# Attention with decay, then a spectral mix, on one core: v loaded with two neighbouring keys per partition

## The chip, the core and the metric

The kernel runs on one core of one Trainium2 chip. The metric is the device time of one launch in microseconds (us). The kernel before the change took 465.24 us (median of three runs, 464.25 to 465.59).

## What is computed

There are two stages. The first is causal attention with a decay, for 8 batches and 8 heads, 576 positions and a head width of 64. The second works on its output x of shape 8 x 576 x 512.

```
scores = scale * q @ k.T                       # per batch and head
cum    = cumsum(log(clip(f, 1e-4, 1)))
scores = where(causal, -1e9, scores + cum[i] - cum[j])
x      = softmax(scores) @ v
X = rfft(x, axis=1); Y = X[:, :64] times (w_r + i*w_i), 512 x 512 per mode
u = x + irfft(Y);  out = u + relu(u @ w_ch)
```

The decay splits into a factor of the query and a factor of the key. The query's factor falls out of the softmax, so the kernel multiplies each row of v by exp(-cum[j]) and carries that weight itself as a 65th column. This column gives the sum that the rows are divided by.

## The kernel before

**Data.** The spectral weights w_r and w_i are 134 MB in HBM. They are cast to bf16 on the way in and make 128 loads of 512 KB at their destination. q, k and v are 9.4 MB each in HBM; q and k are cast, v stays in float32. All loads but f and the first few of v are issued by GpSimd (POOL), which works strictly in the order of the program. At most eight of its loads are under way at once in the trace.

**Pairs.** The attention is worked in 32 pairs (one batch, two heads, `hp` = 0 or 1), one per turn of the loop from L441 on, in a hand-written software pipeline. In turn i:

- POOL issues `load_qk(i + 3)` (L100: one load for q, one for k), `load_v(i + 3)` (L111: one load per head of keys 0 to 511 into `vt`, and for every fourth batch one per head of the last 64 keys of four batches into `vl`), and in most turns `issue_w()` (L140: w_r and w_i of one chunk, 512 KB each). Turns 4, 9, 10, 13 and 21 issue no chunk of w.
- DVE scales v of pair i + 1 (`scale_v`, L304), at the head of the turn.
- TensorE (PE) makes the scores of pair i (`scores`, L319, in parts 0 to 3), multiplies the exponentials of pair i - 1 with v (`av`, L376, blocks 0 to 4), and transposes q and k of pair i + 1 (`trans`, L285). These are interleaved: scores 0, av 0 and 1, scores 1, av 2, trans 0, scores 2, av 3, trans 1, scores 3, av 4. Then come the DFT of pair i - 2 (`dft`, L406) and, from turn 10 on, eight matmuls of one chunk of w (`spec_early`, L424), which frees that chunk's buffer.
- ScalarE (ACT) makes the exponentials of each part of the scores (L346, L333), DVE masks the diagonal blocks (`mask`, L348) and divides (`norm`, L392).

The five key blocks hold 128 consecutive keys each, the last one 64. A diagonal block is masked by the triangle `trimask`. The exponentials of a pair are three tiles of 2 x 512 columns plus a small one for the last block, and both heads' small blocks lie in one tile, heads on different partitions.

**Buffers.** Four of `qk` and of `vt`, two of `vl` (each serves four pairs), seven of w. A load waits until the last reader of its buffer is done.

**After the pairs** a loop over 16 groups of modes takes the remaining chunks of w (L581), each followed by the next `issue_w()`, and the output is made and stored (L634 to L668).

Of the kernel before, what the change touches and what calls it, by code (L numbers as in the profile page):

```python
# [23 lines left out]
def kernel(  # L24
# [11 lines left out]
    nc = tc.nc  # L36
# [34 lines left out]
    trimask = const.tile([128, 128], BF16, name="trimask")  # L71
    tri4 = const.tile([128, 2, 64], BF16, name="tri4")
# [6 lines left out]
    wT = const.tile([128, NPAIR, 9], F32, name="wT")  # L79
# [8 lines left out]
    vspool = actx.enter_context(tc.tile_pool(name="vspool", bufs=3))  # L88
    qtkt = actx.enter_context(tc.tile_pool(name="qtkt", bufs=2))
    epool = actx.enter_context(tc.tile_pool(name="epool", bufs=2))  # L90
# [7 lines left out]
    VG = 4  # L98
# [12 lines left out]
    def load_v(i):  # L111

        g, b = pairs[i]
        vt = vpool.tile([128, 8, Dh], F32, tag="vt", name="vt")
        st[i]["vt"] = vt
        q_v = nc.sync if i < 3 else nc.gpsimd
        for hp in range(2):
            q_v.dma_start(  # L118
                vt[:, 4 * hp : 4 * hp + 4, :],
                v[b, 2 * g + hp, 0:512, :].rearrange("(c p) d -> p c d", p=128),  # L120
            )
        if b % VG == 0:
            vl = vlpool.tile([128, VG, Dh], F32, tag="vl", name="vl")
            for hp in range(2):
                q_v.dma_start(
                    vl[64 * hp : 64 * hp + 64, :, :],
                    v[b : b + VG, 2 * g + hp, 512:576, :].rearrange("b p d -> p b d"),
                )
            for n in range(VG):
                st[i + n]["vl"] = vl[:, n, :]  # L130
# [52 lines left out]
    nc.sync.dma_start(ft, f.rearrange("b h s -> (b h) s"))  # L183
    load_qk(0)
# [6 lines left out]
    masks.make_upper_triangular(nc, trimask[:], val=1.0, diag=True)  # L191
# [35 lines left out]
    nc.vector.tensor_copy(cum[:, S : S + 64], cum[:, 512:576])  # L227
    cps = psM.tile([128, NSB, BH], F32, tag="m", name="cps")
    for sc in range(NSB):
        nc.tensor.transpose(  # L230
            cps[:, sc, :], cum[:, sc * 128 : sc * 128 + 128], ident_f[:BH, :BH]
        )
    for sc in range(4):
        for hp in range(2):
            nc.scalar.activation(
                wT[:, :, 4 * hp + sc].rearrange("p (g b) -> p b g", g=4),
                cps[:, sc, :].rearrange("p (b g hp) -> p b g hp", b=B, g=4)[:, :, :, hp],
                ACT.Exp,
                scale=-1.0,
            )  # L240
    for hp in range(2):
        nc.scalar.activation(
            wT[64 * hp : 64 * hp + 64, :, 8].rearrange("p (g b) -> p b g", g=4),
            cps[64 * hp : 64 * hp + 64, 4, :].rearrange("p (b g hp) -> p b g hp", b=B, g=4)[:, :, :, hp],
            ACT.Exp,
            scale=-1.0,
        )

    def setup_small():
        nc.vector.memset(tri4[:], 0.0)  # L250
        nc.vector.tensor_copy(tri4[0:64, 0, :], trimask[0:64, 0:64])
        nc.vector.tensor_copy(tri4[64:128, 1, :], trimask[64:128, 64:128])
# [51 lines left out]
    def scale_v(i):  # L304
        vs = vspool.tile([128, 9, Dh + 1], BF16, tag="vs", name="vs")
        st[i]["vs"] = vs
        nc.vector.tensor_tensor(  # L307
            vs[:, 0:8, 0:Dh], st[i]["vt"][:], _strided(wT[:, i, 0:8], [[1, 8], [0, Dh]]), ALU.mult
        )
        nc.vector.tensor_scalar(vs[:, 8, 0:Dh], st[i]["vl"], wT[:, i, 8:9], None, ALU.mult)  # L310
        nc.vector.tensor_copy(vs[:, :, Dh : Dh + 1], _strided(wT[:, i, :], [[1, 9], [1, 1]]))
# [3 lines left out]
        [(1, 128, 448, 0), (0, 512, 64, 448)],  # L315
        [(2, 256, 320, 0), (3, 384, 192, 320)],
    ]

    def scores(i, T):  # L319

        QT, KT = st[i]["T"][:, 0, :], st[i]["T"][:, 1, :]
        if T == 0:
            st[i]["et"] = epool.tile([128, 3, 2, 512], BF16, tag="et", name="et")
            st[i]["e4"] = epool.tile([128, 64], BF16, tag="e4", name="e4")
            st[i]["m4"] = epool.tile([128, 2, 64], BF16, tag="m4", name="m4")
        if T == 3:
            ps = psM.tile([128, 64], F32, tag="m", name="s4")
            for hp in range(2):
                sl = slice(64 * hp, 64 * hp + 64)
                nc.tensor.matmul(  # L330
                    ps[sl, :], lhsT=KT[sl, 512:576], rhs=QT[sl, 512:576], start=True, stop=True
                )
            nc.scalar.activation(st[i]["e4"][:], ps[:], ACT.Exp, scale=scale)  # L333
            return
        ps = psS.tile([128, 2, 512], F32, tag="S", name="sps")
        for jb, i0, n, c in SPANS[T]:
            for hp in range(2):
                sl = slice(64 * hp, 64 * hp + 64)
                nc.tensor.matmul(  # L339
                    ps[:, hp, c : c + n],  # L340
                    lhsT=KT[sl, jb * 128 : jb * 128 + 128],
                    rhs=QT[sl, i0 : i0 + n],
                    start=True,
                    stop=True,
                )
        nc.scalar.activation(st[i]["et"][:, T, :, :], ps[:], ACT.Exp, scale=scale)  # L346

    def mask(i, part):  # L348
        et = st[i]["et"]
        if part == 0:  # L350
            d = et[:, 0:2, :, 0:128]
            nc.vector.tensor_tensor(d, d, _strided(trimask[:], [[0, 2], [0, 2], [1, 128]]), ALU.mult)
        else:
            d = _strided(et[:, 2, :, 0:128], [[512, 2], [320, 2], [1, 128]])
            nc.vector.tensor_tensor(d, d, _strided(trimask[:], [[0, 2], [0, 2], [1, 128]]), ALU.mult)
            nc.vector.tensor_tensor(
                st[i]["m4"][:], _strided(st[i]["e4"][:], [[0, 2], [1, 64]]), tri4[:], ALU.mult
            )

    def eblk(i, hp, jb, sb):  # L360

        et = st[i]["et"]
        n = SBLK[sb]
        if jb == 4:
            return st[i]["m4"][:, hp, :]
        if jb == 0:
            T, c = (0, sb * 128) if sb < 4 else (1, 448)
        elif jb == 1:
            T, c = 1, (sb - 1) * 128
        elif jb == 2:  # L370
            T, c = 2, (sb - 2) * 128
        else:
            T, c = 2, 320 + (sb - 3) * 128
        return et[:, T, hp, c : c + n]

    def av(i, sb):  # L376
        if sb in (0, 3):
            st[i]["pav"] = psV.tile([128, 3, 2, Dh + 1], F32, tag="av", name="pav")
        pav, vs = st[i]["pav"], st[i]["vs"]
        Ms = SBLK[sb]  # L380
        for hp in range(2):
            for jb in range(sb + 1):
                rhs = vs[:, 8, :] if jb == 4 else vs[:, 4 * hp + jb, :]
                nc.tensor.matmul(  # L384
                    pav[:Ms, sb % 3, hp, :],
                    lhsT=eblk(i, hp, jb, sb),
                    rhs=rhs,
                    start=(jb == 0),
                    stop=(jb == sb),
                )  # L390

    def norm(i, part):  # L392
        g, b = pairs[i]
        pav = st[i]["pav"]
        for ns, lo, hi in ([(128, 0, 3)] if part == 0 else [(128, 3, 4), (64, 4, 5)]):
            n = hi - lo
            rcp = normsb.tile([128, 3, 2, 1], F32, tag="rcp", name="rcp")
            nc.vector.reciprocal(rcp[:ns, 0:n, :, :], pav[:ns, lo % 3 : lo % 3 + n, :, Dh : Dh + 1])
            nc.vector.tensor_tensor(  # L399
                x_all[:ns, g, b, lo:hi, :].rearrange("p s (h d) -> p s h d", h=2),  # L400
                pav[:ns, lo % 3 : lo % 3 + n, :, 0:Dh],
                _strided(rcp[:ns, 0:n, :, :], [[2, n], [1, 2], [0, Dh]]),
                ALU.mult,
            )
# [33 lines left out]
    scale_v(0)  # L438
    setup_small()
    spec_done = 0  # L440
    for i in range(NPAIR + 2):  # L441
# [6 lines left out]
        if i + 1 < NPAIR:  # L448
            scale_v(i + 1)
        prev = i - 1 if 1 <= i <= NPAIR else None  # L450
        if live:
            scores(i, 0)
        if prev is not None:
            av(prev, 0)
            av(prev, 1)
        if live:
            scores(i, 1)
        if prev is not None:
            av(prev, 2)
            norm(prev, 0)  # L460
        if i + 1 < NPAIR:
            trans(i + 1, 0)
        if live:
            scores(i, 2)
            mask(i, 0)
        if prev is not None:
            av(prev, 3)
        if i + 1 < NPAIR:
            trans(i + 1, 1)
        if live:  # L470
            scores(i, 3)
        if prev is not None:
            av(prev, 4)
            norm(prev, 1)
# [224 lines left out]
```

## Time and profile before

| | |
|---|---|
| time, median of 3 runs | 465.24 us |
| the profiled execution: its own time | 461.9 us |
| its span, first to last instruction | 460.1 us |
| granted TensorE clock over the span | 0.829 |
| PE, DVE, ACT, POOL busy | 75%, 53%, 49%, 42% of the span |
| bytes moved by the DMA engines | 96.64 MB |
| HBM read / written | 163.73 / 9.44 MB |

Shares of busy time are averages over three stretches: the pairs (to about 222 us), the main loop over w (to about 420 us) and the output. The DMA line of the page gives, for 40 equal slices, how busy the 16 DMA engines were in tenths. GB/s counts bytes at the destination, so a cast load counts half of what it reads. In a table of stretches the DMA share can be over 1, because packets overlap on one engine.

### The profile page before, as it was taken

Reading aid. Unit: us, or ns where it says so; the run is one execution under the profiler, and the core shown is the slowest. Engines: PE = TensorE matmul, PEld = TensorE weight load, DVE = VectorE, ACT = ScalarE, POOL = GpSimd, SP = SyncE. Lnnn points to the kernel's source line nnn. Section 1 sums busy time; section 2 is a strip of 40 time slices with the busy share of each in tenths; the row PEclk is TensorE's granted clock in tenths of the full one; section 3 lists DMA queues with packets and bytes.
Section 4 is the critical chain, followed back from the end, with each engine's and each line's share of the span. In section 5 each row is a group of like instructions: output and inputs, shape, how many; then the busy total and the mean of one; then the engine's idle time right before and its main releaser. Section 6 shows DMA issues by size and latency. Waiting matters only on the chain.

```text
span 460.1 us, 8535 instructions
## 1 busy us (share of the span) xinstructions
PE 344.0 (75%) x3396; PEld 169.6 (37%) x3396; DVE 245.2 (53%) x630; ACT 223.4 (49%) x332; POOL 192.3 (42%) x277
## 2 busy tenths in 40 slices
PE   1685897797977769686887479767964787977994
PEld 1353554454544435444433223322331232332331
DVE  7694687797756567677632212111120355533786
ACT  5575466586875658655522022012201354643774
POOL 9654675766566674655432223223232322200000
PEclk9997559798888789778989577577677699988998
DMA  9999999999999999999999999999999999994698
GB/s 167 212 226 212 198 209 225 210 204 190 222 216 210 222 203 223 218 218 218 205 206 206 206 207 206 206 207 206 207 207 206 207 206 207 206 206 70 218 326 279
DMA packets 89319, 96.64 MB, mean 210 GB/s; under 512 B 8288, under 2 KB 82528, under 8 KB 89280
## 3 DMA queue, kind: packets, MB, share of 16 engines
q0 software_dynamic: 80560, 85.61, 107.8%
q1 hardware_dynamic: 8720, 10.50, 7.2%
q8 instruction: 26, 0.43, 0.4%
q14 instruction: 13, 0.11, 0.1%
HBM read 163.73 MB, written 9.44 MB: 376 GB/s over the span
## 4 chain that ended last, share of the span: by engine, by line
DMA 69%; PE 13%; POOL 7%; DVE 5%; issue 5%; DVEq 0%; ACT 0%; POOLq 0%
DMA w<-in_moe_w_i_dram 52%; DMA vt<-in_v_dram 5%; DMA w<-in_moe_w_r_dram 4%; POOL vt L118 3%; DMA x_all<-in_moe_w_i_dram 3%; PE U L645 2%; DMA qk<-in_q_dram 2%; POOL w L152 2%; DMA qk<-in_k_dram 2%; PE Z L645 2%; POOL qk L106 2%; DVE qkT L299 2%; PE pav L384 2%; PE U L651 1%; PE sps L339 1%
## 5 line engine op out<-in xcount | busy, mean ns | idle before, releaser
L346 ACT ACTIVATE et<-sps 128x1024 bf16<-128x1024 f32 x96 | 95.4, 1042 | 19.5 <-PE sps L339 19.3
L152 POOL DMA_DIRECT2D w<-in_moe_w_r_dram x61 | 46.0, 754 | 77.6 <-DMA w<-in_moe_w_r_dram 29.6
L163 PE MATMUL A<-w,XS 128*32 128x512 bf16 x488 | 46.3, 444 | 36.6 <-DMA w<-in_moe_w_i_dram 24.4
L152 POOL DMA_DIRECT2D w<-in_moe_w_i_dram x61 | 46.2, 758 | 63.1 <-DMA w<-in_moe_w_i_dram 58.5
L537 ACT CAST XW<-pxw 128x512 bf16<-128x512 f32 (+1 forms) x40 | 23.3, 584 | 97.2 <-PE pxw L530 97.2
L384 PE MATMUL pav<-vs,et 128*128 128x65 bf16 (+1 forms) x896 | 58.5, 210 | 0.0
L384 PEld LDWEIGHTS <-et 128*128 128x128 bf16 (+1 forms) x896 | 42.2, 111 | 28.4 <-issue 26.4
L299 DVE COPY qkT<-tp 128x640 bf16<-128x640 bf16 x64 | 49.0, 766 | 4.8 <-PE tp L294 4.8
L118 POOL DMA_DIRECT2D vt<-in_v_dram x58 | 45.2, 786 | 11.9 <-DMA w<-in_moe_w_i_dram 3.8
L592 DVE TENSOR_TENSOR Yb<-A,yacc 128x512 bf16<-128x512 f32 x16 | 11.1, 692 | 73.2 <-PE A L163 73.2
L418 ACT CAST XS<-pd 128x192 bf16<-128x192 f32 x32 | 33.2, 1045 | 32.0 <-PE pd L411 31.9
L339 PE MATMUL sps<-qkT 64*128 64x512 bf16 (+4 forms) x320 | 45.0, 347 | 3.9 <-ACT et L346 2.1
L307 DVE TENSOR_TENSOR vs<-vt,wT 128x512 bf16<-128x512 f32 x32 | 22.1, 690 | 47.2 <-DMA vt<-in_v_dram 47.2
L530 PE MATMUL pxw<-wch,xT 128*128 128x512 bf16 (+1 forms) x160 | 46.5, 453 | 0.0
L294 PE MATMUL tp<-ident_bf,qk 128*64 128x128 bf16 x576 | 32.8, 249 | 14.7 <-DMA qk<-in_k_dram 13.1
L399 DVE TENSOR_TENSOR x_all<-pav,rcp 128x384 bf16<-128x384 f32 (+2 forms) x96 | 36.2, 377 | 3.4
L576 DVE TENSOR_TENSOR XW<-pz,XW 128x512 bf16<-128x512 f32 (+1 forms) x40 | 27.0, 690 | 20.2 <-PE pz L575 19.9
L521 DVE COPY xT<-ptr 128x576 bf16<-128x576 bf16 x32 | 14.6, 458 | 36.5 <-PE ptr L516 36.3
L106 POOL DMA_DIRECT2D qk<-in_k_dram x32 | 19.8, 619 | 32.5 <-DMA w<-in_moe_w_i_dram 29.1
L163 PEld LDWEIGHTS <-XS 128*32 128x32 bf16 x512 | 10.3, 96 | 56.7 <-issue 51.1
L662 DVE SCALAR_TENSOR_TENSOR o_sb<-Z,u_sb 128x512 f32<-128x512 f32 (+1 forms) x40 | 25.7, 685 | 8.4 <-ACT u_sb L661 7.5
L294 PEld LDWEIGHTS <-qk 128*64 128x64 bf16 x576 | 21.5, 124 | 20.2 <-DMA qk<-in_q_dram 8.3
(106 smaller groups left out, 502.1 us busy)
## 6 DMA issues: line engine op xcount, KB each, us to landing
w<-in_moe_w_r_dram POOLq DMA_DIRECT2D x61, 512.0 KB, 19.8
w<-in_moe_w_i_dram POOLq DMA_DIRECT2D x61, 512.0 KB, 19.7
out_dram<-o_sb SPq DMA_DIRECT2D x16, 512.0 KB, 3.3
vt<-in_v_dram POOLq DMA_DIRECT2D x58, 128.0 KB, 7.8
qk<-in_q_dram POOLq DMA_DIRECT2D x32, 144.0 KB, 9.6
qk<-in_k_dram POOLq DMA_DIRECT2D x32, 144.0 KB, 8.4
x_all<-in_moe_w_r_dram POOLq DMA_DIRECT2D x3, 512.0 KB, 8.8
x_all<-in_moe_w_i_dram POOLq DMA_DIRECT2D x3, 512.0 KB, 9.9
```

What stands on the lines that cost most here:

```text
L106: nc.gpsimd.dma_start(qk[64 * n : 64 * n + 64, :, :], src[b, 2 * g : 2 * g + 2, :, :].rearrange("h (p r) d -> p h (r d)", p=64),)
L118: q_v.dma_start(vt[:, 4 * hp : 4 * hp + 4, :], v[b, 2 * g + hp, 0:512, :].rearrange("(c p) d -> p c d", p=128),)
L152: nc.gpsimd.dma_start(w8[:, t, :, :], src[4 * u : 4 * u + 4, dc * 128 : (dc + 1) * 128, :].rearrange("m p e -> p m e"),)
L163: nc.tensor.matmul(A[32 * j : 32 * j + 32, :], lhsT=XS[:, dc, c0 : c0 + 32], rhs=w8[:, t, j, :], start=(first and t == 0), stop=(last and ...
L294: nc.tensor.transpose(tp[64 * hp : 64 * hp + 64, r - r0, :, :].rearrange("p n c -> p (n c)"), qk[:, hp, r * 64 : r * 64 + 64], ident_bf[:, :],
L299: nc.vector.tensor_copy(st[i]["T"][:].rearrange("p n (c r) -> p n c r", r=9)[:, :, :, r0:r1], tp[:, 0 : r1 - r0, :, :].rearrange("p r n c ...
L339: nc.tensor.matmul(ps[:, hp, c : c + n], lhsT=KT[sl, jb * 128 : jb * 128 + 128], rhs=QT[sl, i0 : i0 + n], start=True, stop=True,)
L346: nc.scalar.activation(st[i]["et"][:, T, :, :], ps[:], ACT.Exp, scale=scale)
L384: nc.tensor.matmul(pav[:Ms, sb % 3, hp, :], lhsT=eblk(i, hp, jb, sb), rhs=rhs, start=(jb == 0), stop=(jb == sb),)
L399: nc.vector.tensor_tensor(x_all[:ns, g, b, lo:hi, :].rearrange("p s (h d) -> p s h d", h=2), pav[:ns, lo % 3 : lo % 3 + n, :, 0:Dh], _stri ...
L418: nc.scalar.copy(XS[:, g, 0 : 24 * NM].rearrange("p (m c b) -> p c m b", c=3, b=8)[:, :, :, b], pd[:])
L530: nc.tensor.matmul(pxw[:Ms, :], lhsT=xT[:, eb, sb * 128 : sb * 128 + Ms], rhs=wch[:, eb, :], start=(eb == 0), stop=(eb == NEB - 1),)
```

## The change

The keys of v are laid out differently, and the key blocks follow.

- **Loads of v.** Each partition gets two neighbouring keys, so a row of the load is 512 B instead of 256 B: block 0 holds the even keys of 0 to 255, block 1 the odd ones, blocks 2 and 3 the same of 256 to 511. The last 64 keys are loaded for two batches at a time (`VG = 2`), rows of 256 B as before, and both heads go to partitions 64 to 127.
- **Scores.** The weights of a scores matmul are every second column of the transposed k. A block of even or odd keys spans 256 positions, so more columns are computed (3712 instead of 3200 per pair, both heads together). The last keys' block is taken with 128 keys (448 to 575), of which v's rows for the first 64 are zero. It is part of part 2, and the small separate block goes. There are four exponentials per pair: 1024, 1024, 896 and 768 columns.
- **Masks** cover 256 columns of each block (`tri2`), and 64 columns of the last (`trit`).
- **av** has 34 matmuls per pair instead of 30, all 128 rows wide; `norm` divides the last two blocks in one go (four instructions per pair instead of six).
- **Order.** Scores 0 and 1 are put together, then av 0 to 2, both transposes, scores 2 and 3, av 3 and 4. `scale_v(i)` moves into turn i, behind `mask(i, 0)`; before it was done a turn earlier, at the head of turn i - 1.
- The exponentials and the scaled v live in two fixed tiles each (`ets`, `vss`), used in turn, instead of pools of two and three.

```diff
-    VG = 4
+    VG = 2
+    ets = [ssb.tile([128, 4, 2, 512], BF16, name=f"et{n}") for n in range(2)]
+    vss = [ssb.tile([128, 10, Dh + 1], BF16, name=f"vs{n}") for n in range(2)]
...
-                vt[:, 4 * hp : 4 * hp + 4, :],
-                v[b, 2 * g + hp, 0:512, :].rearrange("(c p) d -> p c d", p=128),
+                vt[:, 4 * hp : 4 * hp + 4, :].rearrange("p (s r) d -> p s (r d)", s=2),
+                v[b, 2 * g + hp, 0:512, :].rearrange("(s p r) d -> p s (r d)", s=2, r=2),
...
-            vl = vlpool.tile([128, VG, Dh], F32, tag="vl", name="vl")
+            vl = vlpool.tile([128, VG, 2, Dh], F32, tag="vl", name="vl")
             for hp in range(2):
                 q_v.dma_start(
-                    vl[64 * hp : 64 * hp + 64, :, :],
+                    vl[64:128, :, hp, :],
...
-    masks.make_upper_triangular(nc, trimask[:], val=1.0, diag=True)
+    nc.gpsimd.affine_select(out=tri2[:], in_=tri2[:], ...)
+    nc.gpsimd.affine_select(out=trit[:], in_=trit[:], ...)
...
+    KEYS = [slice(0, 256, 2), slice(1, 256, 2), slice(256, 512, 2), slice(257, 512, 2), TAIL]
     SPANS = [
         [(0, 0, 512, 0)],
-        [(1, 128, 448, 0), (0, 512, 64, 448)],
-        [(2, 256, 320, 0), (3, 384, 192, 320)],
+        [(1, 0, 512, 0)],
+        [(2, 256, 320, 0), (1, 512, 64, 320), (4, 512, 64, 384)],
+        [(3, 256, 320, 0), (0, 512, 64, 320)],
     ]
...
-                    lhsT=KT[sl, jb * 128 : jb * 128 + 128],
+                    lhsT=KT[sl, KEYS[blk]],
...
-            nc.vector.tensor_tensor(d, d, _strided(trimask[:], [[0, 2], [0, 2], [1, 128]]), ALU.mult)
+        d = et[:, 2 * part : 2 * part + 2, :, 0:256]
+        nc.vector.tensor_tensor(d, d, _strided(tri2[:], [[256, 2], [0, 2], [1, 256]]), ALU.mult)
+        if part == 1:
+            d = et[:, 2, :, 384:448]
+            nc.vector.tensor_tensor(d, d, _strided(trit[:], [[0, 2], [1, 64]]), ALU.mult)
...
-        if i + 1 < NPAIR:
-            scale_v(i + 1)
         if live:
             scores(i, 0)
+            scores(i, 1)
         if prev is not None:
             av(prev, 0)
             av(prev, 1)
-        if live:
-            scores(i, 1)
-        if prev is not None:
             av(prev, 2)
             norm(prev, 0)
         if i + 1 < NPAIR:
             trans(i + 1, 0)
+            trans(i + 1, 1)
         if live:
             scores(i, 2)
+            scores(i, 3)
             mask(i, 0)
+            scale_v(i)
         if prev is not None:
             av(prev, 3)
-        if i + 1 < NPAIR:
-            trans(i + 1, 1)
-        if live:
-            scores(i, 3)
-        if prev is not None:
             av(prev, 4)
```

## The prediction

> **What bounds the kernel.** I read the slices, then the chain that ended last, then the table of stretches.
>
> ```profile
> DVE  7694687797756567677632212111120355533786
> DMA  9999999999999999999999999999999999994698
> GB/s 167 212 226 212 198 209 225 210 204 190 222 216 210 222 203 223 218 218 218 205 206 206 206 207 206 206 207 206 207 207 206 207 206 207 206 206 70 218 326 279
> q0 software_dynamic: 80560, 85.61, 107.8%
> DMA 69%; PE 13%; POOL 7%; DVE 5%; issue 5%; DVEq 0%; ACT 0%; POOLq 0%
> ```
>
> The DMA engines are full in every slice up to the 36th; no compute engine is. The chain runs 69% of the span through transfers, nearly all of it w. So until the last chunk of w lands (419.8 us) the span is the sum of transfer times plus the moments in which the DMA engines had too little to do; after that come 40 us of output, which the change does not touch. A microsecond of transfer removed before 215 us is a microsecond of the end, and compute counts only where it starves the DMA engines. The stretches show where that happened:
>
> ```profile
> 90.00:95.00 5.00, 4.58 (x75) 2.84 (x74) 4.82 (x16) 3.79 (x6) 4.97 (x8) 1.00 1.05 182
> 95.00:100.00 5.00, 4.44 (x73) 2.74 (x73) 4.47 (x15) 4.24 (x7) 2.26 (x4) 1.00 1.22 225
> 110.00:115.00 5.00, 3.01 (x35) 1.75 (x33) 4.80 (x15) 1.78 (x4) 5.00 (x8) 0.69 0.89 168
> 165.00:170.00 5.00, 1.88 (x37) 1.45 (x38) 2.89 (x8) 2.29 (x4) 4.87 (x7) 0.99 1.01 178
> ```
>
> The last two columns are DMA share and GB/s; a full stretch has 1.20 to 1.24. The dips (50 to 60, 85 to 95, 105 to 115, 165 to 170) sum to a shortfall of 1.2 stretches' share, about 1.2 / 1.21 x 5 = 5 us. There POOL is busy all the time, and it issues small loads:
>
> ```profile
> 86.12 1.55 POOL L118 DMA_DIRECT2D vt<-in_v_dram  x2 [0.48 <-issue]
> 87.65 0.63 POOL L106 DMA_DIRECT2D qk<-in_q_dram  x1
> 88.25 0.64 POOL L106 DMA_DIRECT2D qk<-in_k_dram  x1
> 88.84 1.60 POOL L118 DMA_DIRECT2D vt<-in_v_dram  x2
> ```
>
> Elsewhere POOL waits for a landing, with seven or eight of its loads under way. The dips sit at turns without a chunk of w: small loads fill the eight places, and issuing one takes as long as moving it.
>
> **What a load of v costs now.** In the trace, where the queue is full, a load lands so long after the one before it: w 2.5 us, q 0.69, k 0.82, first `vt` of a pair 0.46 after k (23 cases), second 0.41 after the first (22), a `vl` about 0.21 (12). So v on POOL's queue takes 58 x 0.433 = 25.1 plus 14 x 0.21 = 2.9, together 28 us.
>
> **What the longer rows save.** The packet records of the trace hold no packets of 256 B on POOL's queue: v goes in 2080 packets of 4096 B, 16 rows each. A quarter of them took 159 ns, the commonest value is 172 ns, the mean 203 ns. The output's packets of 2048 B, one unbroken row each, take 84 ns (median), or 168 ns per 4096 B. The short rows already go almost at the pace of long ones. The changed load will still be packets of 4096 B, of 8 rows. Lower end of the price: two packets per engine and load (128 KB over 16 engines), both at the shortest common 159 ns, 0.318 us instead of 0.433: 58 x 0.115 = 6.7 us saved. Upper end: nothing saved. I take the row nearest, the commonest packet going from 172 to 159 ns: 2 x 13 ns x 58 = 1.5 us, and half of it, since half of the packets are there or have other reasons: **0.8 us**.
>
> The Trainium skill, "DMA: Bandwidth & Descriptors", section Specifications, says the opposite of these rows: at least 512 B per transfer for line rate, below it a read-modify-write. By that rule rows of 512 B might halve v's 28 us, and the forecast would be some 13 us lower. The trace's 159 to 172 ns for 16 short rows speak against it, and I go by the trace.
>
> The first six `vt` loads go by SP's queue, where the records do show 256 B packets: 3584 of them at 23 ns mean (with `vl`), 3584 x 23 / 16 = 5.1 us of one engine each, at 2.7 to 16.3 us. The 3072 of `vt` become 1536 of double size: between 23 ns (half of 4.4 us, 2.2 saved) and 46 ns (nothing). I take a third, **0.7 us**.
>
> **What the extra small loads cost.** `vl` comes every second pair instead of every fourth: 28 loads on POOL instead of 14, of half the size.
>
> ```profile
> L118 POOL DMA_DIRECT2D vt<-in_v_dram x58 | 45.2, 786 | 11.9 <-DMA w<-in_moe_w_i_dram 3.8 <-issue 2.8 <-DVE et L352 1.7
> L125 POOL DMA_DIRECT2D vl<-in_v_dram x14 | 8.7, 627 | 0.5 <-DMA vt<-in_v_dram 0.3 <-DMA qk<-in_k_dram 0.2
> L106 POOL DMA_DIRECT2D qk<-in_q_dram x32 | 19.9, 621 | 17.1 <-DMA w<-in_moe_w_r_dram 6.3 <-PE s L330 3.2 <-PE tp L294 2.8
> ```
>
> POOL: 14 x 0.627 = +8.8 us. A `vt` of 256 rows instead of 512 should lie between 0.627 (a `vl` of 256 rows) and 0.786; at 0.65 that is 58 x 0.136 = -7.9. The total hardly moves, and it matters only in the dips. The one dip that gets a new pair of `vl` is that of turns 9 to 11 (85 to 95 us): +1.25 of issuing, -4 x 0.136 for its four `vt`, +0.7. In the others `vt` gets faster by 0.27 per pair, while `vl` has 0.2 us less to move. I take **+0.5 us** in all; the ends are -1.5 (only the faster `vt` tells) and +3.5 (14 new loads x 0.25 us, from the places that they take).
>
> **The moved `scale_v`.** DVE now waits 47.2 us (20 waits) for `vt` at the head of a turn, with that turn's norm, copies of q and k, and masks queued behind. This wait goes; the next thing late is q and k of pair i + 1, which land 0.5 to 1.5 us before its `vt`. So the turns begin earlier against the loads, but are still paced by them: gain 0. In exchange a buffer of v comes free a turn later. POOL's `load_v(j)` must wait for `scale_v(j - 4)`, behind `mask(j - 4, 0)`. In the trace, POOL's issue of `vt` for pair j came 2.1 us (pair 15) to 12.4 us after that mask plus 0.7, for pair 4 at the same moment. So I count 0 for it. Behind such a wait on POOL stand `vl`, w and the next q and k.
>
> **Compute, behind the transfers.** Per pair, ACT: 3 x 1042 + 228 = 3354 ns become 3842 (slope (1042 - 228) / 960 = 0.85 ns per column): +0.49 us.
>
> ```profile
> L346 ACT ACTIVATE et<-sps 128x1024 bf16<-128x1024 f32 x96 | 95.4, 1042 | 19.5 <-PE sps L339 19.3
> L333 ACT ACTIVATE e<-s 128x64 bf16<-128x64 f32 x32 | 7.3, 228 | 26.7 <-PE s L330 19.6 <-DVE et L352 7.0
> L352 DVE TENSOR_TENSOR et<-et,trimask 128x512 bf16<-128x512 bf16 x32 | 13.3, 417 | 0.4 <-ACT et L346 0.3
> L356 DVE TENSOR_TENSOR m<-e,tri 128x128 bf16<-128x128 bf16 x32 | 6.7, 210 | 0.0
> ```
>
> DVE: masks 417 + 406 + 210 become 2 x 694 + 210 (slope 207 / 384 = 0.54 ns): +0.57; norm loses two instructions, 1649 to 1368 ns: -0.28; scaling the same. PE: 512 more columns, 0.2 us (two matmuls of 512 took 0.39 at full clock), four more av matmuls, 0.24 (six took 0.36): +0.44, twice that at half clock. Weights taken from every second column are not in this trace: between 0 and doubling the 98 ns of 14 loads, 1.4 us a pair, beside matmuls; I take 0, their order lets them overlap. The cover: in the stretch 95 to 105, where nothing waited for data, a turn took 5.1 us; on average it takes 6.66 ((222.1 - 22.4) / 30). With +0.5 us there is 1 us a turn left, so compute stays hidden.
>
> **Start.** POOL builds a mask of 512 columns instead of 128: `trimask` took 0.57 us, so up to 4 x 0.57 = 2.3, plus 0.4, about 2 us before q of pair 2 is issued. The queue then holds w and pair 1 until 16 us. Hidden: 0; if that cover were gone, +2.
>
> **Sum**, against the profiled execution's own 461.9 us (span 460.1): -0.8 - 0.7 + 0.5 = -1.0, 460.9. That execution was 3.3 us under the median of the runs, so I put the forecast on the median: 465.2 - 1.0 = **464.2 us**. About 0.3%, 1.4 us, is what a measurement here can tell from no change.
>
> **Rivals.**
> - *The row length sets the price after all* (that 203 mean against 159 is the short rows). 6.7 + 2.2 us saved, less 0.5: 457, or 457 to 461 when half of it comes. For: the packets' long mean. Against: the 159 ns that a quarter reach with rows of 256 B, and the slow ones bunch where `vl` loads run, whose rows stay 256 B.
> - *The wait for `vl`'s buffer takes the place of DVE's wait* (slower). With two buffers for two pairs each, `vl` for pair j needs `scale_v(j - 3)`, a turn sooner than `vt`. In this trace POOL would be there 1.0 us too early for pair 14, 0.1 for pair 26, and 0.4 to 1.1 us in time for pairs 8, 10, 16, 18; the others have 4. It decides once turns start 1 us later against the loads than now: six pairs, each up to 1.3 us late as compute per turn grows, 6 x 1.3 = 8 at most, half of it covered by loads under way: +4 and the small loads' +0.5, 469; up to 473 when turns are late by the half clock's 0.9 as well. For: w and the next q and k are queued behind. Against: turns start earlier without DVE's wait.
> - *Compute becomes the bound.* If strided weights cost the full 1.4 us and the clock halves often (0.50 from 40 to 65 us), a turn takes 5.1 + 0.5 + 1.4 = 7.0 against 6.66: 30 x 0.35 = +10, some hidden behind seven buffers of w: 468 to 474.
> - *The change doesn't reach the packets*: the row length alters nothing and extra loads cost nothing. That is my forecast within 1 us.
>
> **Chances.** Forecast 0.50 (own range 462 to 466.6: faster 0.20, same 0.30), longer rows 0.18 (faster), `vl`'s buffer 0.22 and compute 0.10 (slower). Faster 0.38, same 0.30, slower 0.32. The range takes in half of the first rival and most of the other two: 459.5 to 469.5 leaves out 0.09 below and 0.09 above.
>
> **What would show it.** Right: packets of 4096 B again, commonest near 159 to 172 ns; `vt` landing steps of 0.38 to 0.43 us; the same dips; no POOL wait on DVE's scaling; DVE's 47 us of waits gone and PE's or DVE's wait for q and k grown. Wrong: `vt` steps near 0.32; POOL idle before `vl` or w until DVE `vs`; PE busy without gaps and DMA share under 1.1 over whole turns; weight loads over 130 ns.

## The result and the profile after

| | before | after |
|---|---|---|
| median of 10 runs each, us | 464.62 (463.81 to 465.59) | 470.21 (466.58 to 473.72) |
| the profiled execution: its own time | 461.9 | 466.58 |
| its span | 460.1 | 464.8 |
| granted TensorE clock | 0.829 | 0.867 |
| the last chunk of w has landed at | 419.7 | 424.6 |
| bytes moved by the DMA engines | 96.64 MB | 96.68 MB |

The ratio is 1.0118, interval [1.0093, 1.0143]: the change costs about 5.5 us. The forecast was 464.2, its range 459.5 to 469.5; the result lies above both. The profiled execution is the fastest of the ten, so its trace shows 4.7 us of it.

First the slices, queue and chain of the page of after (the same lines as were shown of before):

```profile
DVE  7598597798866678676833021202120355553786
DMA  8999999999999999999999999999999999995598
GB/s 154 210 172 213 223 205 227 202 199 190 199 222 211 220 194 205 223 214 226 206 207 206 206 207 206 206 206 206 206 206 206 206 206 207 206 206 85 206 323 287
q0 software_dynamic: 81008, 85.61, 106.8%
DMA 71%; PE 11%; POOL 9%; DVE 4%; issue 4%; ACT 0%; DVEq 0%; POOLq 0%
```

The kernel is bound as before: transfers make 71% of the chain, and the DMA engines are full from the second slice to the 36th. The main loop (from slice 20) shows the same 206 GB/s, so the loss is made before 222 us. The first slice has 154 instead of 167 GB/s, the third 172 instead of 226. To see how it adds up I counted the bytes moved up to a time and divided the difference of the two traces by 206 GB/s. After is 0.9 us behind at 10 and at 25 us, 3.8 at 35, 2.6 to 2.9 up to 90, 4.6 at 130, 5.6 at 200, 5.1 from 222 on. So there are three places: a little at the start, about 3 us between 25 and 35, and the rest slowly from 90 on.

The second place, in the table of stretches of after; the columns are the stretch and its length, busy time of PE, PE's weight loads, DVE, ACT and POOL, granted clock, DMA share, GB/s:

```profile
25.00:30.00 5.00, 3.41 (x70) 2.44 (x68) 4.57 (x13) 3.41 (x5) 3.17 (x5) 1.00 0.65 139
84.00:97.00 13.00, 10.36 (x191) 6.86 (x189) 10.71 (x26) 11.02 (x14) 9.25 (x15) 0.95 0.97 186
117.00:162.00 45.00, 28.86 (x492) 18.18 (x490) 31.37 (x76) 31.38 (x40) 26.88 (x40) 0.92 1.20 213
```

The same three stretches of before:

```profile
25.00:30.00 5.00, 4.33 (x78) 2.94 (x75) 4.90 (x20) 3.70 (x6) 3.24 (x5) 1.00 1.20 226
84.00:97.00 13.00, 11.38 (x158) 6.30 (x157) 9.76 (x32) 9.57 (x13) 10.74 (x16) 0.85 1.08 199
117.00:162.00 45.00, 34.70 (x486) 20.36 (x483) 29.17 (x89) 29.66 (x39) 26.04 (x38) 0.83 1.21 218
```

From 25 to 30 us the DMA share is 0.65 instead of 1.20. POOL's own timeline of after says why (start, length, what, and in brackets the idle time before it with what ended it):

```profile
19.64 0.59 POOL L106 DMA_DIRECT2D qk<-in_k_dram  x1
21.48 1.45 POOL L118 DMA_DIRECT2D vt<-in_v_dram  x2 [1.24 <-DVE vs L314]
26.84 1.20 POOL L125 DMA_DIRECT2D vl<-in_v_dram  x2 [3.92 <-DVE rcp L388]
28.02 0.79 POOL L152 DMA_DIRECT2D x_all<-in_moe_w_r_dram  x1
```

In the kernel before, the same load went behind `vt` at once:

```profile
20.44 1.24 POOL L125 DMA_DIRECT2D vl<-in_v_dram  x2
```

POOL stands still for 3.92 us before the `vl` of pair 4, the third tile for two buffers: it goes into the one that pairs 0 and 1 read, and so waits for `scale_v(1)`, which ends at 26.5 us (the trace names DVE's next instruction, `rcp`). The first load of the chunk of w behind it goes at 28.02 us; with a free buffer it goes at 24.15 (below). This was a rival of the prediction, at a pair which it had taken to be safe.

The loads and masks of after, in the groups by form:

```profile
L118 POOL DMA_DIRECT2D vt<-in_v_dram x58 | 42.2, 735 | 12.6 <-DMA w<-in_moe_w_i_dram 4.5 <-DMA w<-in_moe_w_r_dram 2.5 <-issue 1.8
L125 POOL DMA_DIRECT2D vl<-in_v_dram x28 | 17.0, 619 | 7.3 <-DVE rcp L388 3.9 <-DVE qkT L306 1.1 <-DMA w<-in_moe_w_r_dram 1.0
L355 DVE TENSOR_TENSOR et<-et,tri 128x1024 bf16<-128x1024 bf16 x64 | 43.3, 676 | 0.0
L350 ACT ACTIVATE et<-sps 128x896 bf16<-128x896 f32 x32 | 29.4, 918 | 59.3 <-issue 51.6 <-PE sps L342 4.3 <-ACT et L350 3.4
L342 PEld LDWEIGHTS <-qkT 64*128 64x128 bf16 x448 | 15.0, 104 | 21.9 <-issue 15.1 <-DVE qkT L306 1.7
```

There are 28 `vl` loads, and issuing one of 128 rows takes 619 ns, as much as one of 256 rows before (627): half the size saves nothing here. The masks cost 676 ns (forecast: 694), and the weights from every second column 104 ns instead of 98.

### The profile page after: what moved, and what is told of

Its sections match the earlier page's. It is cut to its first block, busy times and chain, and to the rows that moved or that the text cites. A ratio compares the mean times of both kernels' runs of the same rounds, so it can differ in the third digit from the quotient of the medians.

```text
span 464.8 us, 8942 instructions
## 1 busy us (share of the span) xinstructions
PE 326.7 (70%) x3579; PEld 166.9 (36%) x3588; DVE 262.3 (56%) x572; ACT 233.9 (50%) x332; POOL 196.4 (42%) x291
## 2 busy tenths in 40 slices
DMA packets 88265, 96.68 MB, mean 208 GB/s; under 512 B 5472, under 2 KB 81248, under 8 KB 88224
## 4 chain that ended last, share of the span: by engine, by line
DMA 71%; PE 11%; POOL 9%; DVE 4%; issue 4%; ACT 0%; DVEq 0%; POOLq 0%
DMA w<-in_moe_w_i_dram 57%; DMA qk<-in_k_dram 11%; POOL w L152 3%; POOL qk L106 2%; PE U L628 2%; POOL vt L118 2%; PE Z L628 2%; DMA w<-in_moe_w_r_dram 2%; DMA vl<-in_v_dram 1%; PE U L634 1%; POOL vl L125 1%; DVE et L355 1%; PE pyl L607 1%; PE tp L301 1%; PE pav L374 1%
## 5 line engine op out<-in xcount | busy, mean ns | idle before, releaser
L350 ACT ACTIVATE et<-sps 128x1024 bf16<-128x1024 f32 (+2 forms) x128 | 116.4, 967 | 62.2 <-issue 51.6
L374 PE MATMUL pav<-vs,et 128*128 128x65 bf16 x1088 | 55.1, 205 | 21.4 <-DVE et L355 12.8
L163 PE MATMUL A<-w,XS 128*32 128x512 bf16 x488 | 43.6, 417 | 37.4 <-DMA w<-in_moe_w_i_dram 25.8
L306 DVE COPY qkT<-tp 128x640 bf16<-128x640 bf16 x64 | 46.5, 767 | 39.5 <-PE tp L301 39.5
L374 PEld LDWEIGHTS <-et 128*128 128x128 bf16 x1088 | 45.7, 105 | 44.3 <-issue 21.1
L301 PE MATMUL tp<-ident_bf,qk 128*64 128x128 bf16 x576 | 27.1, 249 | 42.3 <-DMA qk<-in_k_dram 41.6
L118 POOL DMA_DIRECT2D vt<-in_v_dram x58 | 42.2, 735 | 12.6 <-DMA w<-in_moe_w_i_dram 4.5
L342 PE MATMUL sps<-qkT 64*128 64x64 bf16 (+2 forms) x448 | 43.8, 312 | 3.0 <-ACT et L350 1.9
L355 DVE TENSOR_TENSOR et<-et,tri 128x1024 bf16<-128x1024 bf16 x64 | 43.3, 676 | 0.0
L389 DVE TENSOR_TENSOR x_all<-pav,rcp 128x384 bf16<-128x384 f32 x64 | 31.4, 491 | 2.4
```

The lines of the kernel that those rows point to most:

```text
L118: q_v.dma_start(vt[:, 4 * hp : 4 * hp + 4, :].rearrange("p (s r) d -> p s (r d)", s=2), v[b, 2 * g + hp, 0:512, :].rearrange("(s p r) d -> ...
L163: nc.tensor.matmul(A[32 * j : 32 * j + 32, :], lhsT=XS[:, dc, c0 : c0 + 32], rhs=w8[:, t, j, :], start=(first and t == 0), stop=(last and ...
L301: nc.tensor.transpose(tp[64 * hp : 64 * hp + 64, r - r0, :, :].rearrange("p n c -> p (n c)"), qk[:, hp, r * 64 : r * 64 + 64], ident_bf[:, :],
L306: nc.vector.tensor_copy(st[i]["T"][:].rearrange("p n (c r) -> p n c r", r=9)[:, :, :, r0:r1], tp[:, 0 : r1 - r0, :, :].rearrange("p r n c ...
L342: nc.tensor.matmul(ps[:, hp, c : c + n], lhsT=KT[sl, KEYS[blk]], rhs=QT[sl, i0 : i0 + n], start=True, stop=True,)
L350: nc.scalar.activation(ets[i % 2][:, T, :, 0:n], ps[:, :, 0:n], ACT.Exp, scale=scale)
```

## Experiments

The runs came in four groups, each beside runs of the kernel before; where two runs are of different groups, their ratios to the kernel before compare better than their times. A trace holds one execution, and it can lie some us beside the median of its kernel.

**The changed kernel again.** No edit.

> The changed kernel once more, as the base of this group and to see what its slower executions look like, since its profiled execution (466.6 us) was the fastest of ten and the median was 470.2. Expected: 469 to 471 us. Theory W (the wait for the buffer of the last keys): POOL stands idle before a load of the last keys at pair 4, about 4 us, and in a slower execution at further pairs. Theory N (the number of small loads): no such waits beyond pair 4, but more and deeper dips of the DMA share where small loads fill the eight places. Theory C (compute became the bound): turns of over 6.7 us in which PE or DVE has no gap.

469.83 us (467.03 to 472.68), ratio 1.0126 [1.0088, 1.0164]. The loss is the same.

**Is it the buffer?** Four buffers of `vl` instead of two, nothing else:

```diff
-    vlpool = actx.enter_context(tc.tile_pool(name="vlpool", bufs=2))
+    vlpool = actx.enter_context(tc.tile_pool(name="vlpool", bufs=4))
```

> The changed kernel with four buffers for the last keys' loads instead of two, so that such a load waits for scale_v of seven pairs before it and no longer three; the number of loads stays. Theory W: the 3.9 us stall at pair 4 goes; 2.3 us of lost transfer there and whatever the slower executions lose on top come back, 466 us or less. Theories N and C: no more than the 2 us of the start, 468 to 470 us.

467.2 us, 1.0069 [1.0046, 1.0093]: 2.6 us less than the changed kernel beside it (the two intervals overlap a little). POOL's timeline of this run, at the same place:

```profile
21.51 1.44 POOL L118 DMA_DIRECT2D vt<-in_v_dram  x2 [1.27 <-DVE vs L314]
22.93 1.20 POOL L125 DMA_DIRECT2D vl<-in_v_dram  x2
24.15 0.78 POOL L152 DMA_DIRECT2D x_all<-in_moe_w_r_dram  x1
```

`vl` follows `vt` at once, w goes at 24.15 instead of 28.02, and the share from 25 to 30 us is 1.17 instead of 0.65. The wait for the buffer was real, and it is not all: 3 us are still lost.

**Is it the number of small loads?** The last keys are loaded for four batches again, as in before; all other parts of the change stay:

```diff
-    VG = 2
+    VG = 4
```

> The changed kernel with the last keys loaded for four batches at a time again, in two buffers, as before the change: 16 loads instead of 32, and each buffer free a turn later than that of v. Theory W: as with four buffers, 466 us or less, no further gain from the fewer loads. Theory N: 2 to 4 us better than four buffers alone, 463 to 465 us. Theory C: 468 to 470 us.

462.88 us, 0.9973 [0.9948, 0.9998]. That is 6.9 us less than the changed kernel and 4.3 less than with four buffers; the intervals of these two do not touch. So of `VG = 2`, 2.6 us are its buffer and 4.3 us its 14 more loads. Where these 4.3 go, in the stretches of the kernel with four buffers:

```profile
84.00:97.00 13.00, 10.12 (x183) 6.40 (x180) 10.70 (x26) 10.73 (x15) 9.53 (x15) 0.97 1.00 189
117.00:162.00 45.00, 30.73 (x481) 18.70 (x477) 31.52 (x74) 31.34 (x38) 26.90 (x40) 0.85 1.18 212
```

and with `VG = 4`:

```profile
84.00:97.00 13.00, 10.45 (x180) 5.92 (x172) 10.83 (x26) 11.94 (x16) 10.39 (x15) 0.93 1.07 195
117.00:162.00 45.00, 31.40 (x493) 19.79 (x490) 32.48 (x77) 30.27 (x38) 25.78 (x38) 0.84 1.22 222
```

In the dip of 84 to 97 us it is (195 - 189) x 13 = 78 KB, 0.4 us; two traces of the changed kernel differ there by as much (186 and 192 GB/s), so this says little. From 117 to 162 it is (222 - 212) x 45 = 450 KB, 2.2 us, where the share was never low before (the changed kernel's two traces: 213 and 216). The executions traced here, 468.3 and 460.8 us, lie further apart than the medians, so the differences are on the large side. POOL's timelines there differ behind `vl`. With four buffers and a pair of `vl`:

```profile
148.54 1.20 POOL L125 DMA_DIRECT2D vl<-in_v_dram  x2
151.11 0.78 POOL L152 DMA_DIRECT2D w<-in_moe_w_r_dram  x1 [1.36 <-DMA w<-in_moe_w_r_dram]
153.54 0.75 POOL L152 DMA_DIRECT2D w<-in_moe_w_i_dram  x1 [1.65 <-DMA w<-in_moe_w_i_dram]
```

With `VG = 4`, in the same turn:

```profile
150.70 1.44 POOL L118 DMA_DIRECT2D vt<-in_v_dram  x2 [0.44 <-issue]
152.13 0.79 POOL L152 DMA_DIRECT2D w<-in_moe_w_r_dram  x1
152.90 0.78 POOL L152 DMA_DIRECT2D w<-in_moe_w_i_dram  x1
```

Never more than eight loads of POOL are under way, in these traces too. The limit is the program's own: its POOL loads report their landing on eight semaphores, used in strict turn, and in every trace here no load starts until the one eight places before it has landed (by 0.28 us at least). So a `vl` of 32 KB takes one of the eight places just as a load of w with 512 KB does, and behind the pair w waits until an earlier chunk has landed. Between 32 and 205 us, 1607 KB of POOL's loads were under way in the mean with four buffers, and 1817 KB with `VG = 4`.

POOL's time for issuing tells as well. The packet records give the moments in which fewer than 14 packets were being moved by the 16 engines: between 32 and 205 us they add up to 5.9 us in before, 9.4 in after, 9.8 with four buffers and 6.2 with `VG = 4`. In about 9.0 us of the 9.8 POOL was in the middle of issuing a load (4.8 of the 5.9 in before), and in only 0.4 did it stand idle with all eight places taken. So the engines ran low while POOL was at work, with too little under way to cover it; my reading is that places and time of issue work together here. This count is a weak sign of time lost: two traces of one kernel differ by up to 3.3 us in it (2.5 and 5.8, `VG = 4` with `vl` on SP's queue, below).

**`VG = 2` alone, in the kernel before** (with four buffers, so that no wait comes with it):

```diff
-    vlpool = actx.enter_context(tc.tile_pool(name="vlpool", bufs=2))
+    vlpool = actx.enter_context(tc.tile_pool(name="vlpool", bufs=4))
...
-    VG = 4
+    VG = 2
```

> The kernel before, with one edit: the last keys are loaded for two batches at a time (32 loads of half the size instead of 16), in four buffers, so that none waits. Theory N (small loads take the eight places and POOL's time; 467.2 against 462.9 us between four buffers and four batches in the changed kernel): 3 to 5 us slower than before, 467 to 469 us. Rival theory L (not the number, but the start or the buffers): no more than 1 us slower, 464 to 465.5 us.

467.13 us beside 465.05, 1.0056 [1.0025, 1.0086]. The loads alone make the kernel before slower too, by 2 to 3 us. Fewer than 14 packets were being moved for 8.8 us instead of 5.9.

**The last keys off POOL's queue.** If it is the place in POOL's queue and not the bytes, the same 32 loads on SP's queue must be nearly free:

```diff
-    vlpool = actx.enter_context(tc.tile_pool(name="vlpool", bufs=2))
+    vlpool = actx.enter_context(tc.tile_pool(name="vlpool", bufs=4))
...
-                q_v.dma_start(
+                nc.sync.dma_start(
                     vl[64:128, :, hp, :],
```

> The changed kernel with four buffers for the last keys' loads, as in the run at 467.2 us, and these 32 loads issued from SP's queue, so that they take neither POOL's time nor its places. Bytes, sizes and buffers are the same. Theory N: the 4.3 us between four buffers and four batches come back, 462 to 463.5 us. If the many small transfers themselves cost (packets of 2048 B instead of 4096, half the partitions): 466 to 467.5 us.

459.37 us, 0.9875 [0.9838, 0.9913]: 7.8 us less than the same kernel with these loads on POOL, which ran in another group (1.0069); by the ratios it is 9.0. A second time, in another group:

> The changed kernel with four buffers for the last keys and their 32 loads on SP's queue, once more, as the base of this group. Expected 0.986 to 0.992 of before, 458 to 460.5 us.

458.47 us (457.44 to 460.59), 0.9903 [0.9864, 0.9941], by the ratios 7.7 us less. The stretches now:

```profile
84.00:97.00 13.00, 8.81 (x162) 5.41 (x159) 9.82 (x24) 10.40 (x15) 9.61 (x15) 1.00 1.07 199
117.00:162.00 45.00, 31.76 (x492) 19.07 (x490) 32.57 (x79) 31.27 (x40) 24.74 (x36) 0.85 1.22 220
```

Both are back at the pace of before; fewer than 14 packets were being moved for 3.9 us. The loads did not get cheaper for the engines: here each row of 256 B of `vl` goes as a packet of its own, 28 ns in the mean, 3584 x 28 / 16 = 6.3 us of each engine, where POOL's 448 packets of 2048 B took 448 x 121 / 16 = 3.4. This is the fastest version found that leaves nothing out, and it beats both kernels.

**Does the number still matter on SP's queue?** `VG = 4` with `vl` on SP, 16 loads instead of 32, in two comparisons:

```diff
-    VG = 2
+    VG = 4
...
-                q_v.dma_start(
+                nc.sync.dma_start(
                     vl[64:128, :, hp, :],
```

> The changed kernel with the last keys loaded for four batches at a time (two buffers) and these 16 loads on SP's queue: both mends together. Theory N (POOL's places and time are the price, not the transfers): once the loads are off POOL their number costs nothing, so this equals the kernel with 32 loads on SP (0.9875 of before), 0.985 to 0.989, about 459 us. If the number still costs where it stands: 1 to 2 us better than that, 0.983 to 0.985.

> The same with 16 loads of the last keys (four batches at a time, two buffers) on SP's queue, once more, on the same chip as the one with 32. If the number costs only on POOL's queue, the two agree within 0.5%.

459.94 us, 0.9928 [0.9905, 0.9951], and 460.15 us, 0.9933 [0.9906, 0.996]. With 32 loads it was 0.9875 and 0.9903: no loss with twice as many. On POOL the same step cost 4.3 us. So the number costs by POOL's queue, not by the transfers. (With 16 loads there were two buffers, with 32 four.)

**The same in the kernel before:**

```diff
-                q_v.dma_start(
+                nc.sync.dma_start(
                     vl[64 * hp : 64 * hp + 64, :, :],
```

> The kernel before, with one edit: its 16 loads of the last keys go by SP's queue. Theory N: each of the 12 extra pairs of such loads cost about 0.35 us in POOL's order (4.3 us in the changed kernel, some 2.5 in the kernel before), so taking the 7 pairs away gives 1.5 to 2.5 us: 0.9945 to 0.997 of before. If the loads on SP gain by something else (an earlier landing of the last keys): no change here, since DVE's waits in this kernel name vt and not vl.

460.22 us beside 463.51, 0.9925 [0.9897, 0.9953]. Even its 14 small loads on POOL cost 3.3 us. The expectation miscounts: the change adds 7 pairs of such loads, not 12, so its own price is 4.3 / 7 = 0.6 us a pair and 7 pairs would be 4.3 us.

**All of v on SP's queue,** with `VG = 4`:

```diff
-    VG = 2
+    VG = 4
...
-        q_v = nc.sync if i < 3 else nc.gpsimd
+        q_v = nc.sync
```

> The changed kernel with the last keys for four batches at a time and all loads of v on SP's queue, so that POOL issues q, k and w alone. Theory N alone: POOL's dips go, 2 to 4 us better than with only the last keys on SP, 0.979 to 0.983. Against it: on SP's queue the rows go as packets of 512 B at 36 ns instead of 4096 B at 182 ns for eight rows' worth, 256 x 36 / 16 = 0.58 us a load instead of 32 x 182 / 16 = 0.36, 58 x 0.2 = 12 us more transfer; if that decides, slower than 0.99.

466.66 us, 1.0085 [1.0055, 1.0115]: slower, though the DMA engines never ran low (between 32 and 205 us never fewer than 16 packets were being moved). The DMA view of this run (queue: packets, MB, their time as a share of 16 engines' span):

```profile
q0 software_dynamic: 77328, 77.08, 99.5%
q1 hardware_dynamic: 26768, 19.03, 16.6%
```

SP's queue sent every row as a packet of its own. In this run v went in 16384 packets of 512 B at 39 ns mean, 16384 x 39 / 16 = 40.0 us of each engine; on POOL's queue the 58 `vt` loads go in 1856 packets of 4096 B at 182 ns, 21.1 us, with 3.4 us more for the six that SP issues. So this queue suits the small loads, not the large ones.

**What the rows are worth.** The kernel before with rows of 512 B, its other parts unchanged:

```diff
-                vt[:, 4 * hp : 4 * hp + 4, :],
-                v[b, 2 * g + hp, 0:512, :].rearrange("(c p) d -> p c d", p=128),
+                vt[:, 4 * hp : 4 * hp + 4, :].rearrange("p (s r) d -> p s (r d)", s=2),
+                v[b, 2 * g + hp, 0:512, :].rearrange("(s p r) d -> p s (r d)", s=2, r=2),
```

> The kernel before, with one edit: keys 0 to 511 of v are loaded two neighbouring keys per partition, in rows of 512 B; the key blocks stay, so v's rows stand beside the wrong keys and the output differs from the reference. By the changed kernel's loss of 1.9 us when its rows are made short, 1.5 to 2.5 us faster than before: 462 to 463 us. If the gain there came from turns that are arranged otherwise: the same as before.

461.02 us beside 465.05, 0.9914 [0.9879, 0.9949]: 4.0 us saved. And the other way, the changed kernel with rows of 256 B (the edit reversed), then the same in the version with `vl` on SP:

> The changed kernel with the loads of keys 0 to 511 of v in rows of 256 B, as before the change; the rest is untouched, so v's rows stand beside the wrong keys and the output differs from the reference. If the row length is worth what the packets show (commonest 159 ns against 172 ns, a load's issue on POOL 735 ns against 786), this is 1 to 3 us slower than the changed kernel: 471 to 473 us. If longer rows are worth nothing: the same. If they cost (an uneven share of the DMA engines): faster.

> The changed kernel with four buffers and the last keys' loads on SP, and keys 0 to 511 of v in rows of 256 B; v's rows stand beside the wrong keys, the output differs from the reference. If a row's price is POOL's time for issuing (786 against 726 ns, 58 loads, 3.5 us in all) and the packets (172 against 159 ns), 2 to 4 us slower than the run with whole rows. If it was worth something only in the dips, which these loads caused: under 1.5 us.

471.74 us, 1.0163 [1.0132, 1.0194], 1.9 more than the changed kernel, with intervals that overlap; and 462.6 us, 0.9967 [0.9943, 0.9992], 4.1 more than its twin. So the rows give about 4 us. Inside the changed kernel less of it is seen. The group of `vt` with rows of 512 B in the kernel before:

```profile
L118 POOL DMA_DIRECT2D vt<-in_v_dram x58 | 42.2, 734 | 14.7 <-DMA w<-in_moe_w_i_dram 4.2 <-issue 4.2 <-DMA qk<-in_q_dram 1.6
```

Issuing takes 734 instead of 786 ns: 58 x 0.052 = 3.0 us of POOL. In the landing steps, as the prediction read them, the first `vt` comes 0.32 us after k instead of 0.46, the second 0.44 after the first instead of 0.41: 29 x 0.11 = 3.2 us less by the means, and 29 x 0.17 = 4.9 by the medians (0.36 + 0.38 to 0.23 + 0.34). Counted over all 29 pairs it is 0.50 + 0.42 to 0.40 + 0.45, 1.9 us. So the steps alone do not settle it. The traces of the version with `vl` on SP, where POOL's queue has only `vt` in packets of 4096 B, speak for the transfers: with short rows these packets took 209 ns in the mean, with long ones 185, 1856 x 24 / 16 = 2.8 us of each engine, while the engines ran low for about as long (fewer than 14 packets for 3.2 and 3.9 us). In the kernel before the engines even ran low for longer with long rows (10.7 us against 5.9; the traced execution, 463.2 us, is one of the slower). These are single traces, and no run changes the issue alone.

**The moved `scale_v` alone,** in the kernel before:

```diff
-    scale_v(0)
...
-        if i + 1 < NPAIR:
-            scale_v(i + 1)
...
             mask(i, 0)
+            scale_v(i)
```

> The kernel before, with one edit: scale_v(i) is done in turn i behind mask(i, 0) instead of a turn earlier at the head of the turn. DVE's 47 us of waits for v go. If those waits cost anything (turns that begin late, and so buffers that come free late), 1 to 2 us faster; by the prediction's step: no gain, 464 to 465 us. If a later free buffer of v holds POOL: slower, with POOL idle before vt.

464.6 us beside 465.05, 0.9991 [0.9966, 1.0017]: nothing. DVE's wait for `vt` shrank from 47.2 us to 0.5, without a gain.

**Is compute hidden?** The fastest version with every diagonal mask done twice, 64 more masks of 0.68 us:

```diff
         nc.vector.tensor_tensor(d, d, _strided(tri2[:], [[256, 2], [0, 2], [1, 256]]), ALU.mult)
+        nc.vector.tensor_tensor(d, d, _strided(tri2[:], [[256, 2], [0, 2], [1, 256]]), ALU.mult)
```

> The changed kernel with four buffers for the last keys and their loads on SP, and each mask over 256 columns done twice (the mask is zeros and ones, so the result is the same): 2 x 0.69 = 1.4 us more of DVE per pair, five times the 0.28 us that the change added. By the prediction's step (compute lies behind the transfers with about 1 us a turn to spare): 0 to 4 us slower than without, 0.9875 to 0.996. Theory C (compute is the bound in most turns): the whole 32 x 1.4 = 44 us, or near half of it, 1.03 and more.

467.58 us, 1.0103 [1.0073, 1.0134]. It is 9 us slower than the fastest version (458.47; 8 to 11 us by the other pairings), of 44 us of added work (64 x 0.68). In the waits of POOL, up to 215 us, the buffer of `vt` now binds. The first line is of this run, the second of the fastest version (waiter, released by; us in total, times, longest):

```profile
POOL vt L118 <- DVE vs L314: 32.3, 15, 4.2
POOL vt L118 <- DVE vs L314: 2.5, 2, 1.5
```

Then the other side, masks over 128 of the 256 columns, so half of the masking is gone:

```diff
-        d = et[:, 2 * part : 2 * part + 2, :, 0:256]
-        nc.vector.tensor_tensor(d, d, _strided(tri2[:], [[256, 2], [0, 2], [1, 256]]), ALU.mult)
+        d = et[:, 2 * part : 2 * part + 2, :, 0:128]
+        nc.vector.tensor_tensor(d, d, _strided(tri2[:], [[256, 2], [0, 2], [1, 128]]), ALU.mult)
```

> The changed kernel with four buffers and the last keys' loads on SP, with the masks over 128 of the 256 columns of each block: half of the masking is left out, so the output differs from the reference. DVE has 2 x 0.27 = 0.55 us less per pair, less than the kernel before had in all. If the added compute is hidden, within 1 us of the run with whole masks. If it costs in proportion to the doubled masks (some 9 us for 1.36 us per pair), 3 to 4 us faster. If it only costs once DVE is full, the doubled masks' price doesn't carry down: under 1.5 us.

457.85 us, 0.9886 [0.9844, 0.9928]: 0.6 us less than its twin, with intervals that overlap for the most part. At the size of the change, compute on DVE is hidden; at 1.36 us more a pair it is not, and the first to feel it is the buffer that `scale_v` frees.

## Why the prediction was wrong, point by point

Two steps failed. The extra small loads were put at +0.5 us and cost +4.3. The wait for `vl`'s buffer stood in the sum at nothing, and at pair 4, which the prediction took to be in time, it cost +2.6. A third term erred the other way: the longer rows, put at -0.8, gave -4.0 in the kernel before.

**What bounds the kernel: right.** The end moved by about as much as the bytes fell behind before 215 us (span +4.7 us, bytes 5.6 behind at 200 us), and the main loop kept its 206 GB/s. One reading was too broad: of the dips it says that POOL is busy there all the time, but from 50 to 55 and from 105 to 110 us POOL was busy for 3.02 and 2.55 us of 5.

**The extra small loads: the main error, a term mis-sized.** The prediction had +0.5 us, upper end +3.5; the runs show +4.3 in the changed kernel and +2 to +3 in the kernel before. It priced the new `vl` only at the one dip where POOL was busy throughout, at +0.7; there the traces give 0.4, within their spread. It held that elsewhere POOL waits anyway, so that neither its time nor the places cost anything. About half of the loss was made between 117 and 162 us (2.2 us), and when the engines ran low POOL was nearly always issuing (9.0 of 9.8 us), with less under way because small loads stood in the places. The own upper end, 14 x 0.25 us "from the places that they take", was nearer. The step to SP's queue shows how much it is: 7.8 us for 28 loads, about 0.3 us each. That it is POOL's queue, and neither the bytes nor the number of loads, is shown; how much of it is the place and how much the time of issue no run parts.

**The wait for `vl`'s buffer: right as a rival, wrong as to where.** The rival held that `vl` needs `scale_v(j - 3)` and named pairs 14, 26, 8, 10, 16 and 18; "the others have 4" us in time. Of the six only pair 14 waited for it, 0.1 us (pair 10 stood 1.1 us, but with four buffers too). The one that counted was pair 4, for 3.9 us, and it cost 2.6. For pair 4 the prediction had looked at `vt` alone, which needs `scale_v(0)`, and found it due "at the same moment" (it waited 1.2 us); by the rival's own rule `vl` of pair 4 needs `scale_v(1)`, a turn later, so it had to be late by most of a turn. The step that failed is that `vl` of pair 4 was never set against its own releaser. The rival's number, 469 to 473, holds the result, but by a sum that did not happen: it had six waits and +0.5 for the loads.

**The rows: right in sign, too small.** -0.8 us was forecast, -4.0 measured (-1.9 to -4.1 by the other pairs of runs), inside the ends of 0 and -6.7. The packets did what was forecast: 4096 B again, the commonest 159 ns (172 before). The failed step was to price a load by the commonest packet, and then by half. The mean comes nearer: in the kernel before, packets of 4096 B went from 203.6 to 181.9 ns, 2080 x 21.7 / 16 = 2.8 us of each engine, and POOL's issue fell by 3.0 us besides. The prediction laid the slow packets to `vl`, whose rows stay short; but with `vl` off POOL's queue the 1856 packets of `vt` alone still took 198 ns in the mean. So the rival that the row length sets the price was right in part, 4.0 of its 6.7 us. The rule of the Trainium skill, "DMA: Bandwidth & Descriptors", section Specifications, at least 512 B for line rate, has the direction right. The estimate of some 13 us that the prediction made from it was not reached: measured 4. Whether a read-modify-write lies behind it, no run here shows.

**The first six `vt`, -0.7: not seen as a gain.** Their packets did better than forecast: 1536 of 512 B at 36 ns mean, 3.4 us of an engine instead of 4.4. Yet after is 0.9 us behind at 10 us. In that time w is issued earlier and SP loads one more pair of `vl`. What costs the 0.9 was not tried.

**Start, 0: no cost seen.** The mask of 512 columns took POOL 0.62 us, little more than `trimask`'s 0.57, and q of pair 2 was issued at 7.54 us instead of 9.32.

**The moved `scale_v`, 0: right by itself** (0.9991). Together with `VG = 2` and two buffers it is not free: it frees the buffer of `vl` a turn later, and so has its part in the 2.6 us of pair 4. As forecast, the wait went on to q and k. The waits of before (first two lines) and after:

```profile
PE tp L294 <- DMA qk<-in_k_dram: 13.1, 10, 3.0
DVE qkT L299 <- PE tp L294: 4.8, 6, 1.9
PE tp L301 <- DMA qk<-in_k_dram: 41.6, 20, 4.0
DVE qkT L306 <- PE tp L301: 39.5, 22, 4.2
```

**Compute, 0: right.** ACT, DVE and the strided weights cost about what was forecast, and half of the masks is worth nothing measurable. The prediction's reason, a long turn of 6.66 us that covers it, fits, but only for this size: twice the masks cost 9 us.

**What stays open.** Rows -4.0, `VG = 2` +6.9 and `scale_v` 0 make +2.9; measured is 5.5. The remaining 2 to 3 us lie in the rest of the change, or in the rows giving less there (taken out of the changed kernel they were worth 1.9 us, and then the sum is +5.0). `VG = 4` in the changed kernel speaks for the rest: rows alone give -4.0, all but `VG = 2` only -1.3 us by the runs beside it (0.9973). With `vl` on SP and `VG = 4` the changed kernel stands at 0.9928 and before at 0.9925, so there, too, the rest takes back what the rows give. The start's 0.9 us is one part of it. The masks are not (0.6 us). What is left, 1 to 2 us, is within what the intervals leave, and no run here puts it on one part; the order of scores and `av`, the wider scores and the extra `av` matmuls were not tried alone.

## What to carry to other kernels

Where one queue issues everything in order and a fixed number of its loads may be under way, price a small load by what it holds up in that queue, its place and its time of issue, and not by its bytes; try small loads on another queue, and leave the large ones where packets are large. When a change halves how many turns a buffer serves, work out for every tile, the first reuse above all, which instruction frees it, and do so for each kind of tile that the load function fills. When packets of one size have a wide spread of times, price a load by their mean: here it gave 2.8 of the 4.0 us measured, the commonest packet 1.5.

## What the runs showed of the hardware

- A `vl` load of 32 KB cost about 0.3 us more on POOL's queue than on SP's (7.8 us for 28 moved), though at 206 GB/s it moves in 0.16 us. Issuing one took POOL 0.62 us.
- Issuing a load of 128 rows took POOL 619 ns, of 256 rows 627 (`vl`) and 735 (`vt`), of 512 rows 786. Halving the rows of a load saved 1 to 7% of its issue.
- Two queues made different packets of the same load: POOL's took eight rows of 512 B into one packet of 4096 B (182 ns mean), SP's sent each row by itself (36 to 39 ns), 288 to 312 ns for the same bytes.
- DMA engines that never run low are no proof of pace: with all of v on SP's queue they were full throughout, and the kernel took 466.66 us.
